# One transposed load of 256 rows as two of 128, and two plain loads as one, at the head of a gated two-branch mixer

## The chip, the cores and the metric

The kernel runs on one core of one Trainium2 chip. The metric is device time in microseconds (us) of one execution, and the profile gives the span from the first instruction to the last, which is some 1.7 us shorter. In the lines shown, PE is the tensor engine, DVE VectorE, ACT ScalarE, POOL GpSimd, and a q behind a name (SPq: SyncE's) marks the engine's queue issuing a load. A load's slack is the time from its landing to the first instruction that needs it. The chain is the work that ended last, followed back from the last instruction through whatever each step waited for. All results that are compared here come from executions in the fast state (granted clock of the tensor engine 0.998 to 1.0, or a single run next to them in time and clock).

## The reference, cut to what matters

Two branches read the same `x` (2048 rows of 512, bf16) and are blended by a gate per row.

```
x = A_x
g = sigmoid((x * gate_w).sum(-1))
a = linear_attention(x, wqkv, w_phi) @ wo        # softmax features of q and k, kv sums
z = gelu(x @ w_in)                               # 2048 x 1376: z1 | z2
b = (z1 * (w_sp @ layernorm(z2) + b_sp)) @ w_out # w_sp is 2048 x 2048
return g * a + (1 - g) * b
```

`x @ w_in` needs `x` with its 512 features on the partitions, so `x` must be transposed, and needs both halves of `w_in`.

## The kernel before

`x` is handled in 16 tiles of 128 rows. Tiles 0 and 1 are loaded plainly and transposed on the tensor engine (PE), so that PE can start early. The others come transposed by DMA from SyncE's queue. The weight half for z2 comes in four blocks of 128 rows of `w_in`, blocks 0 and 2 on SyncE, 1 and 3 on ScalarE. The half for z1, `w_z1`, comes in two loads.

```python
    nc.sync.dma_start(out=xs[:, 0, :], in_=x2[0:P, :])
    nc.scalar.dma_start(out=xs[:, 1, :], in_=x2[P:2 * P, :])
    load_z2w(nc.sync, 0)
    load_z2w(nc.scalar, 1)
    load_z2w(nc.sync, 2)
    # (gate row on ScalarE) ...
    load_z2w(nc.scalar, 3)
    # ...
    x_dma_T(2, 2)                     # 256 rows: tiles 2 and 3
    for h in range(2):
        nc.sync.dma_start(
            out=w_z1[:, 2 * h:2 * h + 2, :], in_=w_in_v[:, 2 * h:2 * h + 2, 0:FH])
    for i in range(4, 8):
        x_dma_T(i)
    # ... tiles 8 to 15, b_sp, wq/wk transposed, w_phi, value weights, w_sp transposed
```

PE takes the tiles in this order (each tile is 8 matmuls of 344 or 345 columns):

```python
        z2_first_two()                # tiles 0 and 1, all four weight blocks
        z2_tile(2)
        z2_tile(3)
        for c in range(NCH):
            # z2 tiles of chunk c (if c > 0), then its z1 tiles
```

Each DMA issued from SyncE or ScalarE takes one of eight completion semaphores in turn, and waits at its queue until the DMA that had the same semaphore before has landed. This comes from the framework in which the kernel is written; it is in the program's own waits.

The softmax here doesn't subtract the row's maximum and nothing guards it: scores larger than these inputs give would overflow.

## Time and profile before

| what | before |
|---|---|
| time, median of 3 runs (range) | 206.62 us (206.25 to 206.85) |
| span of the profiled execution | 204.5 us |
| PE busy | 98% of the span |
| chain that ended last | 95% PE, 2% DMA |
| the DMA in the chain | block 2 of `w_in`, landed at 6.01 us |

The rows on PE say that it is the bound nearly everywhere; the last one says where a load could still matter, which is only at the start. One caution: the profile of before lacks 18 matmul records, so apparent gaps of 0.43 us from 44 us on in it are missing records.

### The profile page before, as it was taken

The numbers are of one execution on the slowest core, as the hardware profiler recorded it, in microseconds if no ns is written. First come the engines' busy times: TensorE is split into PE (matmuls) and PEld (weight loads), VectorE is DVE, ScalarE is ACT, GpSimd is POOL, SyncE is SP. The second block draws the span as 40 slices with busy tenths as digits, with TensorE's granted clock in tenths as the row PEclk, the third lists the DMA queues.
The fourth block names the chain that finished last, engine by engine and source line by source line (L and its number), as shares of the span: only waits on it lengthen the run. The fifth ranks groups of instructions, "written<-read, shape, count | busy, mean of one in ns | idle before, by whom it ended". The sixth has DMA issues, their size and how long they took to land.

```text
span 204.5 us, 3978 instructions
## 1 busy us (share of the span) xinstructions
PE 199.6 (98%) x1539; PEld 119.7 (59%) x1557; DVE 130.4 (64%) x283; ACT 74.6 (36%) x122; POOL 45.7 (22%) x76
## 2 busy tenths in 40 slices
PE   7999999999999999999999999999999999999994
PEld 3666666655665555656565666555555555665642
DVE  4467484837977587979797789555566645633332
ACT  3466678796222333332424042222351136002303
POOL 3020202021523325334242442222204220200000
PEclk9999999999999999999999999999999999999999
DMA  6997599999998027940422229763568458652833
GB/s 184 269 209 133 118 237 212 239 216 217 235 276 185 3 38 179 290 93 16 75 48 45 51 38 119 139 124 70 100 161 80 90 113 183 63 96 51 156 64 104
DMA packets 89932, 27.22 MB, mean 133 GB/s; under 512 B 84185, under 2 KB 89913, under 8 KB 89913
## 3 DMA queue, kind: packets, MB, share of 16 engines
q1 hardware_dynamic: 87600, 24.81, 63.1%
q10 hardware_dynamic: 2312, 2.16, 3.7%
q8 instruction: 12, 0.20, 0.4%
q14 instruction: 8, 0.06, 0.1%
HBM read 4.15 MB, written 2.10 MB: 31 GB/s over the span
## 4 chain that ended last, share of the span: by engine, by line
PE 95%; DMA 2%; issue 1%; SPq 0%; DVE 0%
PE mm L454 37%; PE zp L191 18%; PE mm L355 13%; PE mm L515 8%; PE mm L395 7%; PE mm L509 7%; DMA w_z<-in_B_w_in_dram 2%; PE kvacc L411 2%; PE at L467 2%; PE mm L520 1%; PE zp L307 0%; PE at L478 0%; SPq L117 0%; SPq L119 0%; PE pq L307 0%
## 5 line engine op out<-in xcount | busy, mean ns | idle before, releaser
L454 PE MATMUL mm<-z2all,wspT 128*128 128x344 bf16 x512 | 79.9, 309 | 0.0
L454 PEld LDWEIGHTS <-wspT 128*128 128x128 bf16 x512 | 49.0, 98 | 25.3
L191 PE MATMUL zp<-w_z,xT 128*128 128x344 bf16 (+1 forms) x254 | 38.1, 310 | 0.3 <-DMA w_z<-in_B_w_in_dram 0.3
L359 ACT ACTIVATE eq<-mm 128x512 bf16<-128x512 f32 x32 | 17.4, 594 | 51.4 <-PE mm L355 25.7
L363 DVE TENSOR_REDUCE zs<-eq 128x64 f32<-128x1024 bf16 x16 | 19.5, 1220 | 20.0 <-ACT eq L359 20.0
L191 PEld LDWEIGHTS <-xT 128*128 128x128 bf16 x254 | 24.4, 98 | 12.1 <-issue 0.3
L359 ACT ACTIVATE ek<-mm 128x512 bf16<-128x512 f32 x32 | 17.3, 601 | 27.1 <-PE mm L355 27.1
L459 DVE SCALAR_TENSOR_TENSOR ucat<-mm,bT,z1all 128x344 bf16<-128x344 f32 x32 | 17.4, 544 | 15.1 <-PE mm L454 15.1
L372 POOL TENSOR_TENSOR eq<-eq,ratio 128x512 bf16<-128x512 bf16 x16 | 16.9, 1055 | 44.6 <-DVE ratio L371 36.6
L531 ACT ACTIVATE ob<-mm,g_inv 128x512 bf16<-128x512 f32 (+1 forms) x15 | 10.1, 679 | 33.1 <-PE mm L520 28.5
L363 DVE TENSOR_REDUCE zs<-ek 128x64 f32<-128x1024 bf16 x16 | 19.2, 1208 | 2.8 <-ACT ek L359 2.8
L515 PE MATMUL mm<-wspT,uT 128*128 128x512 bf16 (+2 forms) x85 | 20.1, 367 | 0.0
L355 PEld LDWEIGHTS <-xT 128*128 128x128 bf16 x128 | 12.2, 98 | 12.0
L372 POOL TENSOR_TENSOR ek<-ek,ratio 128x512 bf16<-128x512 bf16 x16 | 16.9, 1055 | 2.2 <-DVE ratio L371 1.7
L395 PE MATMUL mm<-wv_sb,xT 128*128 128x512 bf16 x64 | 16.4, 380 | 0.0
L355 PE MATMUL mm<-wq_p,xT 128*128 128x512 bf16 x56 | 16.0, 380 | 0.4
L355 PE MATMUL mm<-wk_p,xT 128*128 128x512 bf16 x61 | 16.1, 379 | 0.2
L509 PE MATMUL mm<-wspT,oT 128*128 128x512 bf16 (+2 forms) x61 | 15.6, 365 | 0.4
L209 DVE BATCH_NORM_STATS2 bn<-z2all 128x6 f32<-128x344 bf16 x32 | 14.9, 502 | 0.0
L206 ACT ACTIVATE z2all<-zp 128x688 bf16<-128x688 f32 x16 | 11.8, 743 | 7.6 <-PE zp L191 7.6
L260 ACT ACTIVATE z1all<-zp 128x688 bf16<-128x688 f32 x16 | 11.9, 743 | 5.1 <-PE zp L191 4.7
L515 PEld LDWEIGHTS <-uT 128*128 128x128 bf16 x85 | 8.1, 98 | 9.4 <-issue 0.2
(77 smaller groups left out, 142.0 us busy)
## 6 DMA issues: line engine op xcount, KB each, us to landing
out_dram<-ob ACTq DMA_DIRECT2D x12, 128.0 KB, 2.4
wspT<-in_B_w_out_dram SPq DMA_DIRECT2D x2, 640.0 KB, 4.9
w_z<-in_B_w_in_dram SPq DMA_DIRECT2D x2, 344.0 KB, 5.0
wv_sb<-in_A_wqkv_dram SPq DMA_DIRECT2D x2, 256.0 KB, 4.4
wspT<-in_A_wo_dram SPq DMA_DIRECT2D x2, 256.0 KB, 3.9
out_dram<-ob SPq DMA_DIRECT2D x3, 128.0 KB, 1.8
w_z<-in_B_w_in_dram ACTq DMA_DIRECT2D x2, 172.0 KB, 3.7
w_z<-in_B_w_in_dram SPq DMA_DIRECT2D x2, 172.0 KB, 3.8
```

What stands on the lines that cost most here:

```text
L191: nc.tensor.matmul(zp[:, j, 0:n], lhsT=xT[:, dt, tt * P:(tt + 1) * P], rhs=wt[:, dt, j * HF:j * HF + n], start=(dt == 0), stop=(dt == NDT ...
L209: nc.vector.bn_stats(out=bn6[:, tt, j, :], in_=z2v[:, j, :])
L260: nc.scalar.activation(out=z1all[:, tt, :].rearrange("p (j n) -> p j n", j=2), in_=zp[:, :, 0:HF], func=AF.Gelu_apprx_tanh,)
L355: nc.tensor.matmul(ps[:, :], lhsT=xT[:, dt, tt * P:(tt + 1) * P], rhs=w[:, dt, :], start=(dt == 0), stop=(dt == NDT - 1))
L359: nc.scalar.activation(out=e[:, :, a, :], in_=ps[:, :].rearrange("p (h f) -> p h f", f=DH), func=AF.Exp, scale=1.0 - 2.0 * a)
L363: nc.vector.tensor_reduce(out=z[:].rearrange("p h a -> p (h a)"), in_=e[:].rearrange("p h a f -> p (h a) f"), axis=AX.X, op=ALU.add,)
L372: nc.gpsimd.tensor_tensor(out=e[:, :, 1, :], in0=e[:, :, 1, :], in1=ratio[:, :, None].to_broadcast([P, H, DH]), op=ALU.mult)
L395: nc.tensor.matmul(v_ps[:, :], lhsT=xT[:, dt, tt * P:(tt + 1) * P], rhs=wv_sb[:, dt, :], start=(dt == 0), stop=(dt == NDT - 1))
L454: nc.tensor.matmul(gp[:, 0:HF], lhsT=wspT[:, st, tt * P:(tt + 1) * P], rhs=z2all[:, st, j * HF:(j + 1) * HF], start=(st == 0), stop=(st == ...
L459: nc.vector.scalar_tensor_tensor(out=ucat[tt % NU][:, c0 + j * HF:c0 + (j + 1) * HF], in0=gp[:, 0:HF], scalar=bT[:, tt:tt + 1], in1=z1all[ ...
L509: nc.tensor.matmul(acc, lhsT=oTs[tt][:, g, :], rhs=wo_t[:, g, c0:c1], start=start and g == 0, stop=stop and g == NG - 1)
L515: nc.tensor.matmul(acc, lhsT=uTs[tt][:, i + ft, :], rhs=w_main[i][:, ft, c0:c1], start=start and ft == 0, stop=False)
```

## The change

The intent is to let x tile 2 arrive without waiting for tile 3, and to spare one issue for the value weights.

```diff
-    x_dma_T(2, 2)
+    x_dma_T(2)
+    x_dma_T(3)
```

```diff
-    for h in range(2):
-        nc.sync.dma_start(
-            out=wv_sb[:, 2 * h:2 * h + 2, :],
-            in_=A_wqkv[h * 2 * P:(h + 1) * 2 * P, 2 * D:3 * D].rearrange("(dt p) n -> p dt n", p=P),
-        )
+    nc.sync.dma_start(out=wv_sb[:, :, :], in_=A_wqkv[:, 2 * D:3 * D].rearrange("(dt p) n -> p dt n", p=P))
```

The order of the instructions on PE, VectorE, ScalarE and GpSimd is untouched; some of them wait for another semaphore of the eight.

## The prediction

> **What bounds the kernel now.** I read the page first, then the chain of waits from the start, then the DMA issue queue of SyncE in order of time, then each early load's time to landing.
>
> The page (busy time, slices, chain that ended last):
>
> ```profile
> PE 199.6 (98%) x1539; PEld 119.7 (59%) x1557; DVE 130.4 (64%) x283; ACT 74.6 (36%) x122; POOL 45.7 (22%) x76
> ...
> PE   7999999999999999999999999999999999999994
> ...
> DMA  6997599999998027940422229763568458652833
> ...
> PE 95%; DMA 2%; issue 1%; SPq 0%; DVE 0%
> ```
>
> The tensor engine is full in 38 of 40 slices and 95% of the chain is its own work. The loads touched by the diff can only act where the chain is not PE: the 2% under DMA, all at the start. There the DMA engines are busy too (6 9 9 7 in slices of 5.1 us).
>
> The chain in order of time (start us, length us, what):
>
> ```profile
> 1.72 4.29 DMA w_z<-in_B_w_in_dram
> 6.01 0.04 issue
> 6.05 0.45 PE zp L191 x2
> 6.51 0.32 PE zp L191 x2
> 6.83 16.96 PE zp L191 x116
> 23.80 2.36 PE zp L191 x16
> 26.15 0.12 PE zp L307 x2
> ```
>
> The one load in the chain is block 2 of the w_in half for z2, issued at 1.72 and landed at 6.01. From 6.05 on PE runs without a gap: 16.96 us / 116 = 0.146 us a matmul of 344 columns. So I can count when each later load is needed. After block 2 come 8 such matmuls and two one-column ones of about 0.03 (blocks 2 and 3 of tiles 0 and 1): 6.05 + 8 x 0.146 + 0.05 = **7.27 for x tile 2**. Eight more: **8.44 for x tile 3**; eight more: **9.61 for the first half of w_z1** (row blocks 0 and 1), four more: **10.19 for its second half**. x tile 4 follows four z1 tiles of 8 matmuls: **14.28**. The fold of the phi weights starts at **26.15**.
>
> What SyncE issues (start us, length us, line, operation):
>
> ```profile
> 1.26 0.88 SPq L117 DMA_DIRECT2D w_z<-in_B_w_in_dram  x2
> 2.18 1.43 SPq L131 DMA_TRANSPOSE xT<-in_A_x_dram  x1
> 3.67 1.08 SPq L135 DMA_DIRECT2D w_z<-in_B_w_in_dram  x2
> 4.79 5.12 SPq L131 DMA_TRANSPOSE xT<-in_A_x_dram  x4
> 9.96 4.41 SPq L140 DMA_TRANSPOSE xT<-in_A_x_dram  x2
> 17.51 4.13 SPq L150 DMA_DIRECT2D wphi<-in_A_w_phi_dram  x8
> 23.56 1.10 SPq L152 DMA_DIRECT2D wv_sb<-in_A_wqkv_dram  x2
> ```
>
> The second row is the 256-row load to be split; the fourth shows what a 128-row one costs the queue, 5.12 / 4 = 1.28 us.
>
> Time from issue to landing (last column), asked for narrow windows: the 256-row load, then the first w_z1 half:
>
> ```profile
> xT<-in_A_x_dram SPq DMA_TRANSPOSE x1, 5.0
> w_z<-in_B_w_in_dram SPq DMA_DIRECT2D x1, 344.0 KB, 4.8
> ```
>
> x tiles 2 and 3 land at 2.18 + 5.0, about 7.15, only 0.1 us ahead of the need at 7.27: close, but not waited for. The first w_z1 half lands at 3.67 + 4.8 = 8.5 (slack 1.1). The second, issued at 4.28 with 5.1 to landing by the same line's spread, lands at 9.4 (slack 0.8).
>
> **What the Trainium skill says.** (1) "DMA: Bandwidth & Descriptors", section "Queues, rings and completion order": an engine takes descriptors in ring order, and a load's completion is written only after the earlier writes of that DMA engine. The trace agrees with the order: blocks 0 and 2, the transposed load and the two w_z1 halves land in the order of their issue. (2) Same page, "Rules for kernel authors": small transfers are to be coalesced. The trace agrees for issue time: two 128-row transposes would take 2 x 1.28 against 1.43. (3) "Perfetto Trace Analysis", "DMA Optimizations": splitting lets part of the work start sooner if the DMA engines are generally idle. Here they are not, so I expect little of it. (4) Same page, "Summary: the profiler window per engine type": the row of such a DMA is its issue, the data movement comes later. The trace agrees (1.43 us against 5.0 to landing), so I judge by landings.
>
> **The change part by part.** The program's instruction order on PE, DVE, ACT and POOL is the same in both kernels, as far as lines are concerned; only which completion semaphore some of them wait for changes. On SyncE one transpose becomes two, and two plain loads become one. Blocks 2 and 3 of w_in keep their queues and places, so the words about them in the change describe what is there already.
>
> *Split of the x load.* Bytes are the same (256 KB). The queue pays 2 x 1.28 in place of 3.67 - 2.18 = 1.49: **+1.07 us for everything behind it**, up to the value weights. The second transpose also reuses the semaphore of x tile 1's load on ScalarE (issued at 0.80, 2.7 to landing: 3.5), and its turn comes at 3.46, so that adds under 0.05. What it gives: tile 2 no longer waits for tile 3's rows and should land a few tenths before 7.15. That is slack, as PE is held by block 2 until 6.05 and has work until 7.27.
>
> *What the 1.07 us meets.* x tile 3: issued near 3.5 and behind the same data as before, landing 7.2 to 7.6, need 8.44. First w_z1 half: issued at 4.74 instead of 3.67. If the whole delay reached the landing it would be 9.55, need 9.61. Second half: 5.35 + 5.1 = 10.45, need 10.19, **a stall of 0.26 at worst**. But the landing is set by the data ahead more than by the issue: the DMA engines are busy until past 10 us, the half cannot start before the x rows are in (7.15), and it will have been issued over two us before that. So I expect 8.5 to 9.0 and 9.4 to 9.9, and no stall. x tiles 4 to 7: four issues from 5.86, the last landing near 12.7 (8.65 + 2.9 + 1.1), need 14.28 for the first and 3 x 1.17 later for the last. Last phi block: issued by 21.64, 1.6 to landing, plus 1.07: 23.9 to 24.3, need 26.15. Nothing waits.
>
> *Value weights in one load.* One issue less: about -0.5 (1.10 for two, the first w_z1 half of similar kind took 0.57). The spatial weights' transposes then issue at 24.70 + 1.07 - 0.5, near 25.3; the first lands 0.6 later, near 37.9, while its first matmul is at 46.48 by the chain. The value weights themselves are needed from 45.6 and land before 30. Off the path.
>
> *Sum.* Removed from the path: nothing certain. Added: 0 to 0.26. Central estimate 0, so 206.6.
>
> **The rivals.** (a) *The later w_z1 issue becomes a wait.* For: its slack, 0.8 and 1.1, is about the shift. Against: the queue of data in front. If it comes, +0.1 to +0.3, 206.9. (b) *Block 2 lands sooner.* PE stood idle for about 0.25 us before 6.05 waiting for it. The transposed rows share the DMA engines with blocks 2 and 3, and half as many are now handed over at once. If that thins the contention, block 2 comes up to 0.25 earlier, 206.4. Against: block 2 is ahead of them in its ring. (c) *Tile 2 was nearly late, so landing earlier pays.* Only if block 2 also comes sooner; alone it gives 0. (d) *The shift reaches later phases* through transposes of u and exp(q): those are issued after the spatial weights and consumed far later; their order is the same. 0.
>
> **Range and chances.** Every way that I can size is within 0.3 us of 206.62; the three runs of the kernel before spread by 0.6. Adding them gives 206.1 to 207.1. 2% is 4.1 us, more than the whole DMA share of the chain minus its unavoidable part could give, and ten times the worst stall found: faster 0.005, slower 0.01.
>
> **What would show it right or wrong.** In the changed profile: two transposes of about 1.2 us each, w_z1 issued near 4.75 (+1.07); the first value-weight row near 24.6 and the spatial weights near 25.3; PE's rows without a gap at 7.27, 8.44, 9.61 and 10.19 counted from block 2's landing; block 2 landing within 0.2 of 6.01; the chain 95% PE. The prediction fails if a wait on w_z1 or on xT appears in the chain, if the transposes slow blocks 2 or 3 by over 0.5 us, or if an unpredicted wait appears past 46 us.

## The result, and the profile after

| | before | changed |
|---|---|---|
| median of 6 runs | 206.45 us | 206.23 us |
| range | 205.94 to 206.85 | 205.98 to 206.93 |
| ratio | | 0.9997, 95% interval 0.9973 to 1.0021 |
| span of the profiled execution | 204.5 us | 204.3 us |

A ratio is the mean time of one kernel's fast runs over that of the other's fast runs of the same rounds, so it is not quite the ratio of the medians.

The page of the changed kernel: PE's busy time, and the chain by engine.

```profile
PE 200.5 (98%) x1557; PEld 119.7 (59%) x1557; DVE 130.4 (64%) x283; ACT 74.6 (37%) x122; POOL 45.6 (22%) x76
...
PE 94%; DMA 4%; SPq 1%; DVE 0%; issue 0%
```

PE is as full as before, and the DMA share of the chain is larger. But the chain is another one. In order of time (start us, length us, what):

```profile
0.80 2.88 DMA xs<-in_A_x_dram
...
3.70 1.19 SPq L131
...
4.93 0.59 SPq L136
...
5.57 4.34 DMA w_z<-in_B_w_in_dram
...
9.96 13.59 PE zp L188 x92
```

Before, the chain began with a wait for block 2 of `w_in` (its issue at 1.72), and PE ran from 6.05 without a gap. Here it is read as follows. x tile 1's plain load lands at 3.68 and frees a semaphore; only then is the second transposed piece issued (3.70); behind it stand the two `w_z1` loads, the second issued at 5.57 and landed at 9.91; and PE, which would have been ready at 9.70 (its previous matmul started at 9.55, and one takes 0.146), starts the matmul that needs it at 9.96. So **a wait of 0.26 us on `w_z1` came in**. At the same time the wait of 0.25 us on block 2 is gone.

SyncE's queue (start us, length us, line, operation), to be held against the rows shown of before:

```profile
2.20 2.69 SPq L131 DMA_TRANSPOSE xT<-in_A_x_dram  x2
4.93 1.10 SPq L136 DMA_DIRECT2D w_z<-in_B_w_in_dram  x2
6.08 5.13 SPq L131 DMA_TRANSPOSE xT<-in_A_x_dram  x4
...
25.61 0.58 SPq L152 DMA_DIRECT2D wv_sb<-in_A_wqkv_dram  x1
26.24 36.26 SPq L154 DMA_TRANSPOSE wspT<-in_B_w_sp_dram  x4
```

The two pieces hold the queue until 4.89, the one load held it to 3.61: the first `w_z1` half is issued at 4.93 instead of 3.67. The value weights cost 0.58 instead of 1.10.

Times from issue to landing (last column): block 2 of `w_in`, x tile 2, x tile 3, the second `w_z1` half.

```profile
w_z<-in_B_w_in_dram SPq DMA_DIRECT2D x1, 172.0 KB, 3.2
...
xT<-in_A_x_dram SPq DMA_TRANSPOSE x1, 4.0
...
xT<-in_A_x_dram SPq DMA_TRANSPOSE x1, 3.1
...
w_z<-in_B_w_in_dram SPq DMA_DIRECT2D x1, 344.0 KB, 4.3
```

Block 2, issued at 1.73, landed at 4.96, 1.05 us earlier than in the profile of before. x tile 2 landed at 6.23 and tile 3 at 6.78. The `w_z1` half was issued 1.29 us later than before but landed only 0.49 us later, as its time to landing fell from 5.1 to 4.3.

Does anything differ later? The chain's first piece of the k projection and its last piece, before and then changed:

```profile
43.89 0.21 PE mm L355
...
201.74 0.35 DVE ob L527
```

```profile
43.65 1.73 PE mm L352 x8
...
201.51 0.35 DVE ob L524
```

201.74 - 43.89 = 157.85 and 201.51 - 43.65 = 157.86. The two executions are the same from 44 us on; their whole difference, 0.24 us, arises before. The same subtraction gives 157.86 or 157.87 in each of the further profiles at full clock. So the study can be reduced to one question: when does PE get through the first 10 us?

The two waits named above all but cancel, so there is a third term. It is block 0 of `w_in`, which PE needs first: it landed at 4.57 before and at 4.30 in the changed kernel, and PE's first `w_in` matmul moved with it (before, then changed):

```profile
4.61 0.31 PE L191 MATMUL zp<-w_z,xT 128*128 128x344 bf16 x1 [0.25 <-DMA w_z<-in_B_w_in_dram]
```

```profile
4.34 0.31 PE L188 MATMUL zp<-w_z,xT 128*128 128x344 bf16 x1
```

So PE is 0.27 us ahead by its earlier start, 0.50 once block 2 needs no wait either, and 0.24 after the wait on `w_z1`. Block 0 is issued at 1.26 in both kernels, before anything that the change touches.

### The profile page after: what moved, and what is told of

The parts are those of the page before. It is cut to its first block, busy times and chain, and to the rows that moved or that the text cites. A ratio compares the mean times of both kernels' runs of the same rounds, so it can differ in the third digit from the quotient of the medians.

```text
span 204.3 us, 3996 instructions
## 1 busy us (share of the span) xinstructions
PE 200.5 (98%) x1557; PEld 119.7 (59%) x1557; DVE 130.4 (64%) x283; ACT 74.6 (37%) x122; POOL 45.6 (22%) x76
## 4 chain that ended last, share of the span: by engine, by line
PE 94%; DMA 4%; SPq 1%; DVE 0%; issue 0%
PE mm L451 37%; PE zp L188 16%; PE mm L352 14%; PE mm L512 9%; PE mm L506 7%; PE mm L392 7%; DMA w_z<-in_B_w_in_dram 2%; PE kvacc L408 2%; PE at L464 2%; DMA xs<-in_A_x_dram 1%; PE mm L517 1%; SPq L131 1%; PE zp L304 0%; SPq L136 0%; PE at L475 0%; PE pq L304 0%
## 5 line engine op out<-in xcount | busy, mean ns | idle before, releaser
L451 PEld LDWEIGHTS <-wspT 128*128 128x128 bf16 x512 | 49.0, 98 | 25.3
L506 PE MATMUL mm<-wspT,oT 128*128 128x512 bf16 (+2 forms) x68 | 16.6, 366 | 0.0
```

Source lines behind the costliest of these rows:

```text
L451: nc.tensor.matmul(gp[:, 0:HF], lhsT=wspT[:, st, tt * P:(tt + 1) * P], rhs=z2all[:, st, j * HF:(j + 1) * HF], start=(st == 0), stop=(st == ...
L506: nc.tensor.matmul(acc, lhsT=oTs[tt][:, g, :], rhs=wo_t[:, g, c0:c1], start=start and g == 0, stop=stop and g == NG - 1)
```

## The experiments

Two things had to be explained: the wait on `w_z1` that came in, and the wait on block 2 that went out. **Theory A**: both are effects of the split: the later issue delays `w_z1`, and the smaller transposed load leaves blocks 2 and 3 more of the DMA engines. **Theory B**: the first is an effect of the split, the second is scatter from execution to execution. Twelve runs were made (four of them of the two kernels as they are), all with correct results.

### Both kernels again, and each part alone

The first two kernels have no edit. The third has only the first hunk of the diff, the fourth only the second.

> The kernel before, unchanged, profiled a second time. Theory A (the split itself lets block 2 of w_in land sooner): block 2 lands near 6.0 us again and the matmul that needs it waits about 0.25 us, first wait-free matmul of block 2 at 6.0 to 6.1. Theory B (block 2's landing is scatter between executions): it can land anywhere from 4.9 to 6.1. Both: second half of w_z1 issued near 4.28, landed near 9.4, no stall there. Time 206 to 207.

> The changed kernel, unchanged, profiled a second time. Theory A: block 2 lands near 5.0 again, no wait for it. Theory B: it lands anywhere from 4.9 to 6.1. Both: w_z1 halves issued near 4.9 and 5.5, the second lands near 9.9, a stall of 0.1 to 0.4 us at the matmul that needs it unless the start was late. Time 206 to 207.

> Only the split of the x load, value weights in two loads as before. Both theories: w_z1 issued near 4.9 and 5.5, second half lands near 9.9, stall 0.1 to 0.4 us. A: block 2 near 5.0. B: anywhere from 4.9 to 6.1. The first spatial-weight transpose issues about 0.5 us later than in the changed kernel (near 26.7), which nothing waits for. Time 206 to 207.

> Only the value weights in one load; one 256-row transposed load as before. Both theories: w_z1 issued near 3.7 and 4.3, landed by 9.5, no stall on it. A: block 2 near 6.0 with a wait of 0.25 us. B: anywhere from 4.9 to 6.1. First spatial-weight transpose near 24.2, 0.5 us earlier than before, and no effect on the end. Time 206 to 207.

Measured: 205.96, 206.73, 206.29 and 206.12 us (one run each), beside 206.06 for the kernel before on that chip. The landings are in the table further down. Unsplit, the second `w_z1` half lands at 9.56 and 9.61; split, at 9.57 and 9.93. Neither of the two split profiles has the wait on it: for the split alone, where 0.1 to 0.4 us was expected, that is a miss. PE was late for other reasons. In the changed kernel's second profile block 0 of `w_in`, which PE needs first, landed at 5.22 instead of 4.30:

```profile
1.26 3.96 DMA w_z<-in_B_w_in_dram
...
5.26 0.31 PE zp L188
...
7.33 16.96 PE zp L188 x116
```

PE began 0.9 us later than in the first profile and had no wait on block 2, `xT` or `w_z1`. In the profile of the split alone the chain contains no DMA at all; its first two `w_in` matmuls took 0.29 us each:

```profile
4.66 0.29 PE zp L192
4.95 0.29 PE zp L231
5.24 0.31 PE zp L192 x2
```

A start-to-start time of 287 ns for 344 columns, in place of 145, is what the Trainium skill describes in "TensorE: Matmul & The Clock Gate", section "Part 1: The HAM clock gate": an array that has not yet been let up to full clock takes N / 1.2 GHz (344 / 1.2 = 287 ns), and how many matmuls that hits varies by run. The trace agrees in the durations (286 and 287 ns); its record of the granted clock reads 1.00 there, so that the array was cold is inferred from the durations alone. No effect of the change is needed for it: the third profile of the kernel before shows it too.

What follows: of the split profiles with the loads in this order, only the one in which PE was early has the wait on `w_z1`. The single load of value weights does what was said of it (from their issue to that of the first spatial-weight transpose, 24.08 to 24.71 in its kernel, against 23.56 to 24.70 in the kernel before: 0.63 instead of 1.14 us), and nothing waits for that.

### Is it the issue time? Remove the delay, exaggerate it, have it without the split

The second half of `w_z1` from ScalarE:

```diff
-        nc.sync.dma_start(
+        (nc.sync, nc.scalar)[h].dma_start(
             out=w_z1[:, 2 * h:2 * h + 2, :], in_=w_in_v[:, 2 * h:2 * h + 2, 0:FH])
```

> The changed kernel with the second half of w_z1 issued from ScalarE (behind its table load) instead of SyncE. If the 0.25 us stall on that half comes from its late issue: issued near 4.6 instead of 5.5, landed at or before 9.5 instead of 9.9, no stall of the matmul that needs it, and PE limited by block 2 or by the start alone. Rival (the data rate sets the landing, whatever the issue): lands at 9.8 to 10 all the same. Time 205.7 to 206.6.

Measured: 207.12 us, **a miss**. The half was issued at 4.67 as expected and landed at 9.62, but the *first* half, still on SyncE, landed at 10.44, and x tile 3 took 5.2 us to land where it took 3.1 to 3.8 in the four split profiles. The chain in time, and tile 3's landing:

```profile
4.95 5.49 DMA w_z<-in_B_w_in_dram
...
10.48 14.19 PE zp L188 x96
```

```profile
xT<-in_A_x_dram SPq DMA_TRANSPOSE x1, 5.2
```

PE waited until 10.48 for the first half (0.36 us). Issued from the other queue, the second half shared the DMA engines with the transposed rows: from 6.0 to 7.2 us the trace has 47 packets of ScalarE's queue and 218 of SyncE's, 0.11 MB in all, and the 47 took 72.5% of the 16 engines' time, some 0.30 us each; in the changed kernel, from 7.2 to 9.0 us, 637 packets took 102.3%, some 0.05 us each. Tile 3 landed at 8.89, the second half at 9.62, and the first half, which PE needs before the second, last. In this kernel x tile 1's copy on ScalarE also comes later, at 5.09 instead of about 4.4, because the issue stands before it; so it isn't a clean removal of the delay alone.

Four transposed loads of 64 rows:

```diff
-    x_dma_T(2)
-    x_dma_T(3)
+    for c in range(4):
+        nc.sync.dma_start_transpose(
+            out=xT[:, :, 2 * P + 64 * c:2 * P + 64 * c + 64],
+            in_=x2[2 * P + 64 * c:2 * P + 64 * c + 64, :])
```

> The changed kernel with the 256 rows in four transposed loads of 64 rows. Issue theory: each piece costs the queue 1.1 to 1.2 us, so w_z1 issues near 7.1 and 7.7 (plus waits for the semaphores that the pieces reuse), its halves land near 10.8 and 11.8, and PE stalls for 1.5 to 2.5 us on them: time 207.5 to 208.5. Rival (issue time is hidden by data already queued): landings stay below 10, time 206 to 207. Contention theory for block 2: it lands within 0.9 us of block 0, as the pieces come later still.

Measured: 208.16 us, inside the expected range. Its chain in order of time:

```profile
3.67 1.17 SPq L134
...
4.89 1.25 SPq L134
...
6.18 1.25 SPq L134
...
8.10 3.76 DMA w_z<-in_B_w_in_dram
...
11.91 13.59 PE zp L190 x92
```

Each 64-row piece holds the queue as long as a 128-row one. `w_z1` was issued at 7.47 and 8.10 and landed at 10.85 and 11.86. The rival, that issue time is hidden by queued data, is true for a delay of one microsecond and false for one of four: the time from issue to landing of the second half goes 5.1 (issued 4.28), 4.3 (5.57), 3.76 (8.10), so each further delay is hidden less. PE waited 0.83 and 0.42 us for the two halves, 1.25 together, less than the 1.5 to 2.5 expected, and 0.49 for tile 3. The expectation about block 2 was missed: it landed 1.61 us behind block 0, not within 0.9.

One 256-row load, but two tiny plain loads before `w_z1`:

```diff
     x_dma_T(2, 2)
+    spare = early.tile([P, 2, 64], BF16, name="spare")
+    for k in range(2):
+        nc.sync.dma_start(out=spare[0:16, k, :], in_=x2[0:16, 0:64])
```

(The pieces are 2 KB each, not 4 KB as the expectation says.)

> The kernel before with its one 256-row load, and two tiny plain loads (4 KB each) put between it and w_z1, so that w_z1 issues near 4.6 and 5.2 as in the changed kernel, without the split. If the issue time alone moves the landing: second half lands near 9.9 and PE stalls there, unless block 2 already held PE back. If the split's data order matters instead: it lands near 9.5. Block 2: 1.4 to 1.6 us behind block 0, as in the three unsplit profiles so far, since the 256-row load stands in the same place. Time 206 to 207.

> The one 256-row load with w_z1 delayed by two tiny loads, a second profile. First time its second half was issued at 5.34 and landed at 9.59. If the late issue alone makes the landing late: 9.7 to 9.9 this time and a stall if PE started early. If the order of the rows matters: 9.5 to 9.6 again. Block 2 minus block 0 was 0.90; near 1.5 now if the first was an outlier. Time 206 to 207.

Measured: 206.36 and 206.63 us. The second half was issued at 5.34 and 5.15, and landed at 9.59 and 9.74. On average that lies between unsplit and split, as its issue does. PE did not wait for it: it was held up before, by the gate's row in the first profile and by slow first matmuls in the second. Block 2 landed 0.90 and 0.88 us behind block 0, where 1.4 to 1.6 was expected: a miss.

The 256-row load behind both `w_z1` halves:

```diff
-    x_dma_T(2, 2)
     for h in range(2):
         nc.sync.dma_start(
             out=w_z1[:, 2 * h:2 * h + 2, :], in_=w_in_v[:, 2 * h:2 * h + 2, 0:FH])
+    x_dma_T(2, 2)
```

> The kernel before with the 256-row transposed load put behind both w_z1 halves. If the transposed rows slow blocks 2 and 3 down, block 2 now lands 0.4 to 0.7 us behind block 0 (unsplit so far 1.4 to 1.6, split 0.7 to 1.3); if its lateness is only the bytes ahead of it, it stays 1.0 to 1.6 behind. x tiles 2 and 3 come late here (near 9 to 9.5), so PE stalls some 2 to 2.5 us for tile 2: time 208 to 209. The interest is in block 2's landing, not in the time.

Measured: 208.77 us. PE waited for x tile 2:

```profile
4.05 5.70 DMA xT<-in_A_x_dram
...
9.80 16.53 PE zp L191 x112
```

Block 2 landed at 6.55, 2.21 us behind block 0, outside both expected ranges. With the transposed rows taken away from behind it, it came **later**, not earlier. That speaks against the part of theory A by which the transposed rows slow blocks 2 and 3, but it does not refute it: the `w_z1` halves took their place right behind block 2, and it is one profile.

### Timed, and the last profiles

No edits: the changed kernel, the split alone, the kernel before.

> The changed kernel once more, timed in five rounds and profiled a third time. So far its second w_z1 half landed at 9.91 and 9.57 (split alone: 9.93), against 9.42, 9.56 and 9.61 unsplit. Issue theory: 9.7 to 10.0 again. Block 2 minus block 0 so far 0.66, 1.03, 1.28 split and 1.44, 1.55, 1.42 unsplit, but 0.90 in the unsplit kernel with delayed w_z1 and 1.61 with four pieces; if scatter, anything from 0.6 to 1.6 can come. Ratio to before 0.998 to 1.003, verdict same.

> The split alone (two loads of value weights), timed in five rounds and profiled a second time. If the single load of value weights is worth nothing, the same as the changed kernel: second w_z1 half lands at 9.7 to 10.0, time from the first matmul of the next phase (line of the k projection) to the end 160.8 us as in every profile so far, ratio to before 0.998 to 1.003.

> The kernel before, a third profile. Issue theory: second w_z1 half lands at 9.4 to 9.6. Block 2 minus block 0: 1.4 to 1.6 if the gap belongs to the unsplit load, anything from 0.6 to 1.6 if it is scatter. Time 205.9 to 206.9.

Measured: the changed kernel's four fast runs took 206.10 to 206.53 us, ratio 0.9985 (0.9972 to 0.9998); its fifth, the profiled one, ran at a granted clock of 0.559 and took 355.76 us, so it gives no third comparable profile. (In it the second `w_z1` half, issued at 5.75, landed at 9.48, where 9.7 to 10.0 was expected, and block 2 came 1.02 us behind block 0.) The split alone: 206.60 us, ratio 1.0007 (0.9990 to 1.0023). The kernel before: 206.62 us (11 runs), and 206.32 in the run that was profiled.

The profiles that bear on these two loads in one table, in us from the start, read from the traces (the two kernels with `w_z1` moved to another queue or place are left out; the runs were on different chips, 3 for the first eight and 5 for the last four):

| kernel | block 0 / block 2 landed | difference | second `w_z1` half: issued | landed | PE waits for it | first k matmul |
|---|---|---|---|---|---|---|
| before | 4.57 / 6.01 | 1.44 | 4.28 | 9.42 | 0 | 43.73 |
| before, second | 4.19 / 5.74 | 1.55 | 4.18 | 9.56 | 0 | 43.46 |
| value weights only | 4.34 / 5.76 | 1.42 | 4.18 | 9.61 | 0 | 43.55 |
| before, third | 4.38 / 6.09 | 1.72 | 4.21 | 9.30 | 0 | 43.81 |
| delay without split | 4.43 / 5.33 | 0.90 | 5.34 | 9.59 | 0 | 43.70 |
| the same, second | 4.18 / 5.07 | 0.88 | 5.15 | 9.74 | 0 | 43.95 |
| changed | 4.30 / 4.96 | 0.66 | 5.57 | 9.91 | 0.26 | 43.49 |
| changed, second | 5.22 / 6.25 | 1.03 | 5.46 | 9.57 | 0 | 44.23 |
| split only | 4.33 / 5.61 | 1.28 | 5.63 | 9.93 | 0 | 43.65 |
| split only, second | 4.34 / 6.04 | 1.70 | 5.65 | 9.92 | 0 | 43.76 |
| four pieces | 4.37 / 5.98 | 1.61 | 8.10 | 11.86 | 0.42 | 45.44 |

(With four pieces PE also waited for tile 3 and for the first half.)

What follows for **`w_z1`**. Four unsplit profiles: issued at 4.21 and landed at 9.47 on average. Four split ones: 5.58 and 9.83. An issue 1.37 us later gave a landing 0.36 us later. With the delay alone, 5.25 and 9.67: 1.03 us gave 0.20. At that rate the delay of the split kernels would give 0.26 of their 0.36. So the later issue explains most of the later landing, and roughly three quarters of the delay is hidden. The samples are small and overlap (one split landing at 9.57, one unsplit at 9.61), so a small effect of the row order is not excluded.

The traces also show where the rest of the delay comes out. In the changed profile the transposed rows were through early (tile 3 landed at 6.78), and from 6.5 to 7.0 us the DMA engines moved only 55 GB/s before the rows of `w_z1` came; with the split alone (6.88) it was 72. In the four unsplit profiles, with `w_z1` already queued, they moved 217 to 318 in that stretch, with the delay alone 146 and 243. In the other two split profiles tile 3 landed at 7.30 and 7.36 and there was no such gap (156 and 276): there the landing was set by the data in front.

What follows for **block 2**. Split profiles give 0.66 to 1.70 us behind block 0, unsplit ones 1.42 to 1.72. On average the split ones are earlier by 0.36 us, but one split profile (1.70) is all but as late as the latest unsplit one, and block 0 itself scatters by a microsecond. (The split kernel with half of `w_z1` on ScalarE gave 1.01.) Most split profiles are thus earlier, which leans towards an effect of the split, but the kernel with a delay and no split was as early. A second idea, that it is `w_z1`, not the transposed rows, that slows block 2 when issued early, fits the kernel with `w_z1` right behind block 2 (2.21) and the two delayed ones (0.90, 0.88), and fails on four pieces (1.61, with `w_z1` issued at 7.47) and on the second profile of the split alone (1.70). The cause stays open. Neither A nor B is shown for it.

What follows for the **time**. First k matmul at 43.64 on average unsplit, 43.78 split, with scatter of 0.35 and 0.74 between executions of each. The three timed comparisons of kernels with the split, 0.9997, 0.9985 and 1.0007, fall on either side of 1 (the interval of the second just leaves 1 out, those of the others do not). Whether a tenth of a per cent is left is not settled by these runs; 2% is far away. No experiment pointed to a version that beats both: in the profiles of the two kernels the largest wait on block 2, `xT` or `w_z1` is 0.3 us, 0.15% of the time. Block 0's landing scattered by more (PE began 0.9 us later for it in one profile), but it is issued before all that was changed.

## Why the prediction was right, point by point

**PE is the bound, loads matter only before 10 us: right.** The stretch from the k projection to the last piece of the chain was 157.85 to 157.87 us in each profile at full clock.

**"+1.07 us for everything behind it": right in kind, too small.** The first `w_z1` half went from 3.67 to 4.93, +1.26. The missing part is the semaphore: "that adds under 0.05" was mis-sized. x tile 1's load landed at 3.68 instead of 3.49, and the second piece went out at 3.70 where it could have at about 3.53: 0.17 us; in the two profiles of the split alone it was 0.24 and 0.26, in the changed kernel's second 0.03. Later on the shift also grew: b_sp's issue came at 16.50 instead of 14.48. The prediction put the first spatial-weight transpose at 25.3 and its landing near 37.9; it came at 26.24 and landed at 40.55, as its time to landing also grew, from 12.6 to 14.3. Nothing waits for it: its first matmul in the chain is at 46.24.

**"8.5 to 9.0 and 9.4 to 9.9, and no stall": landings right, the stall right only in part.** They landed at 8.84 and 9.91. In the profiled execution there was a stall of 0.26, in the three other comparable profiles with the split there was none. By the prediction's own list of signs it failed here, as a wait on `w_z1` appears in the chain. The step that failed is the need at 10.19: it was counted from block 2's landing at 6.01, and with blocks 0 and 2 landed at 4.30 and 4.96 PE was ready at 9.70. Rival (a) and rival (b) were treated as alternatives; in this execution both came, and the second brought on the first: PE was early, therefore it had to wait. That the worst case of 0.26 was also the measured wait is a coincidence, since it came from a landing at 10.45 and a need at 10.19.

**x tile 2 a few tenths earlier, tile 3 at 7.2 to 7.6, both slack: right on the slack.** They landed at 6.23 and 6.78 in the profile, earlier than said, and at 6.37 to 6.88 and 6.88 to 7.36 in the three others; no wait on them.

**Block 2 "within 0.2 of 6.01": not so in the profile** (4.96); with block 0's earlier landing it is what made the changed profile look better at its head. The four profiles of the split rows spread from 0.66 to 1.70 us behind block 0, so scatter is at least a part of it.

**Value weights, -0.5, off the path: right** (1.10 to 0.58, no effect on the end).

**The sum, 206.6 with 206.1 to 207.1: right.** 206.23 in the first six runs, 206.10 to 206.53 in the four fast ones later, against 206.45 and 206.62. That the profiled execution came out so near is in part luck: three terms of about 0.25 us, of which the prediction had counted on none, happened to leave 0.24.

## What to carry to other kernels

Splitting a load can help where something waits for the whole of it; here nothing did. What it costs is paid by the loads behind it in the same queue, so count their slack first, one by one, from the landing to the first matmul that reads them. While the DMA engines still had queued data, most of an issue delay was hidden (1.37 us later gave a landing 0.36 later); past that it was not (2.52 us more, with four pieces, gave 2.03 more). Before explaining a difference of 0.2 us between two profiles, profile the unchanged kernel again: here its own start moved by more.

## What the Trainium skill lacked or had wrong

- "DMA: Bandwidth & Descriptors", sections on the DMA transpose: no time in us for *issuing* a transposed load by its row count (only a count of sequencer cycles for small tiles, in the part on a later build). Measured on SyncE at the head of this kernel: 1.17 to 1.27 us for 64 rows, 1.19 to 1.32 for 128, 1.33 to 1.43 for 256, so that up to 256 rows it is almost a fixed price. (In the one profile where these loads stood behind `w_z1`, it was up to 1.51 for 128 rows and 1.79 for 256.)
- "DMA: Bandwidth & Descriptors", "Rules for kernel authors", says that a transpose next to ordinary DMAs needs nothing. It speaks of correctness, and the results here were correct; no time is given for a transposed load with another queue's rows beside it. Here a 128-row one with 344 KB of plain rows from ScalarE's queue beside it took 5.2 us to land (one profile), where it took 3.1 to 3.8 without.
- "Perfetto Trace Analysis", "DMA Optimizations", says that splitting may let some transfers start sooner if the DMA engines are idle. It lacks the price for those behind: two pieces delayed the next load's issue by 1.26 us, of which 0.17 was a wait for a reused completion semaphore (0.03 to 0.26 in the four split profiles); over four profiles of each kind the landing of the load after that was delayed by about a quarter of its issue's delay.
- No page gives the scatter of early landings between executions of one kernel: in two profiles of the changed kernel block 0 landed at 4.30 and 5.22 us; in two of the split alone block 2 came 1.28 and 1.70 us after it.
- "TensorE: Matmul & The Clock Gate" describes the cold clock at a kernel's start, which agrees (287 ns for 344 columns). A whole execution at a mean clock of 0.559, 355.76 us instead of 206.1, came once in these runs of a kernel on one core; the page tells of a gate stuck for 50 us and of a limit with three busy cores, not of this.
